# A decode block with TensorE's program in three blocks: all 32 units in its loop, queries by a loop over heads, the last matmuls in block one

## The chip, the cores and the metric

The kernel runs on one core of a Trainium2 chip. A core has five engines that run their own instruction streams and meet at semaphores: TensorE (PE, matmuls; its weight loads are listed as PEld), VectorE (DVE), ScalarE (ACT), GpSimd (POOL) and SyncE (SP), which here issues nearly all transfers from HBM into SBUF. The metric is the device time of one execution in microseconds (us); less is better.

## The reference

One step of decoding for a batch of two: attention over a cache of 8192 keys in 32 heads, and then a gated feed-forward block. All numbers are float32.

```python
# x (2,1,512); k_cache, v_cache (2,32,8192,128); wq (512,4096); wo (4096,512)
# w_gate, w_up (512,1792); w_down (1792,512)
def attention(x, k_cache, v_cache, wq, wo):
    q = (x @ wq).reshape(B, 1, 32, 128).transpose(0, 2, 1, 3)
    scores = einsum("bhqd,bhkd->bhqk", q, k_cache) * 128 ** -0.5
    o = einsum("bhqk,bhkd->bhqd", softmax(scores), v_cache)
    return o.transpose(0, 2, 1, 3).reshape(B, 1, 4096) @ wo
def ffn(x, w_gate, w_up, w_down):
    return (silu(x @ w_gate) * (x @ w_up)) @ w_down
h = x + attention(layernorm(x), k_cache, v_cache, wq, wo)
out = h + ffn(layernorm(h), w_gate, w_up, w_down)
```

## The kernel before, in words

**Units and slots.** The cache is worked through in U = 32 units; a unit is two heads of one batch row, so 8192 KB of keys and 8192 KB of values, laid out as 128 rows of 64 KB. Three SBUF tiles of that size hold them: `kslot0` and `kslot1` for keys in turn, `vslot` for values. Below, k5 means the keys of unit 5 and v5 its values. VectorE multiplies a unit's keys by the query (L471) and sums them to scores (L475), in halves, and takes the maximum (L478). TensorE and ScalarE make the softmax of it (L409 to L413, L502, L506). TensorE multiplies the values by the probabilities `pz` with 32 matmuls into `opart` (L418), ScalarE copies that out (L519), and four more matmuls and a copy give a column of `oT` (L430, L523).

**Who issues what.** The list `loads` is written in the order in which SP issues: wq, k0 (two halves), k1, v0, k2, v1, ... k31, v30, v31, wo (two parts), w_gate, w_up (two parts), w_down (five parts). Before the first part of an item SP waits for what stands in `after`: the release of the tile that the item is written to. `s_kfree` counts units whose keys VectorE has used, `s_vfree` units whose values TensorE has used (ScalarE adds to it, L518). SP issues in order, so whatever stands behind a waiting item waits too. TensorE starts on values when the whole load has landed.

**The last unit.** v30 goes to `vslot` as all values before it. v31 goes to `kslot0` (`v_last`), which is free once VectorE is through with k30. wo follows into `vslot`, after v30 is used; w_gate and w_up go to `kslot1`, after k31; w_down goes to `kslot0`, after v31. For this TensorE's loop has 31 turns, and unit 31 stands behind it as code of its own.

**Queries.** wq lands in `vslot`. The transposed and normalised x (`hT`, 32 columns) is multiplied with it in 32 matmuls (L362), four at a time in four groups of columns; ScalarE copies the two results out (L374); eight matmuls with the constant `picks` (L384) spread them over the partitions, and ScalarE copies each into `qsb` (L397). VectorE starts on k0 after the first of these copies; SP may issue v0 once L362 is through.

**The end.** TensorE multiplies `oq` by wo (32 matmuls, L578), then comes the residual, the second layernorm, w_gate and w_up (L612), and w_down in 14 chunks: eight into `early` (L690), chunks 8 to 13 with four small matmuls each (L658), and four that add `early` (L675). VectorE and ScalarE copy the result out, SP and ScalarE store it.

**Branches of TensorE.** The functions `tour`, `stops`, `far_stop` and `last` write blocks of code to which TensorE jumps at the start (`tour`: to `stop1`, `stop2`, and back to `toured`) or at its end (`back`); they compute nothing.

Of the kernel before, what the change touches and what calls it, by code (L numbers as in the profile page):

```python
# [11 lines left out]
P = 128  # L12
# [42 lines left out]
def decode_block(nc, x, k_cache, v_cache, wq, wo, w_gate, w_up, w_down, out):  # L55
# [43 lines left out]
    quarter = sbuf("quarter", P, NQ)  # L99
    picks = sbuf("picks", P, 2, B, P)  # L100
    om = picks[:, 0].rearrange("p b (h q) -> p b h q", q=NQ)
    sides = sbuf("sides", P, P // (2 * W), 2 * W)
    pz = sbuf("pz", P, NW, 2 * W)
    oT = sbuf("oT", P, H, B)
    hT = sbuf("hT", P, DC, 32)
    osb = sbuf("osb", P, W * DH)
    qsb = sbuf("qsb", P, B, MQ, DH)
    oq = sbuf("oq", P, H, B)
# [36 lines left out]
    def alone(name):  # L145
        return g.sem(name)
# [10 lines left out]

    v_last = kslot[U % 2]

    def load_kv(kind, i, parts=1):  # L160
        cache, t = (k_cache, kslot[i % 2]) if kind == "k" else (v_cache, vslot if i < U - 1 else v_last)
        n = SLOT // parts
        for c in range(parts):
            own = parts > 1 or (kind, i) == ("v", U - 1)
            sem = alone(f"{kind}{i}_{c}") if own else s_k[i % 2] if kind == "k" else s_v
            loads.append(((kind, i), c, t[:, c * n : (c + 1) * n], k_src(cache, i)[:, c * n : (c + 1) * n], sem))
# [8 lines left out]

    wo_t = vslot
    WO = ((0, 20), (20, 12))
# [11 lines left out]
    for e, (c, n) in enumerate(WF):  # L189
# [6 lines left out]
        ))  # L196
    wd_t = v_last
    WD = ((0, 4), (4, 4), (8, 3), (11, 2), (13, 1))
# [8 lines left out]
    for item, e, dst, src, sem in loads:  # L207
        count[sem] = count.get(sem, 0) + 16
        landed[item, e] = (sem, count[sem])
    after = {("v", 0): ("wq", 0), ("wo", 0): ("v", U - 2), ("wf", 0): ("k", U - 1), ("wd", 0): ("v", U - 1)}  # L210
    for i in range(1, U):
        after["v", i] = ("v", i - 1) if i < U - 1 else ("k", U - 2)
        if i > 1:
            after["k", i] = ("k", i - 2)
# [4 lines left out]
    def tour(e):  # L219
        e.br("stop1")  # L220
        never["reg"] = e.alloc_register("never")
        nc.switch_bb("toured", parent=None)

    def stops(e):
        e.br("past1")
        with nc.body("stop1", parent=None, valid_engines=[PE]):
            e.reg_mov(never["reg"], 0)
            never["hint"] = e.mark_branch_hint_location()
            e.br("stop2")
        with nc.body("back", parent=None, valid_engines=[PE]):  # L230
            e.nop()
            e.br("end")
        nc.switch_bb("past1")

    def far_stop(e):
        e.br("past2")
        with nc.body("stop2", parent=None, valid_engines=[PE]):
            e.nop()
            e.br_lt(never["reg"], 1, "toured", "past2").branch_hint(never["hint"])
        nc.switch_bb("past2", parent=None)  # L240

    g.steps["tensor"].append(tour)
    def keep(name, engine):
        held = {}

        def mark(e):
            held["reg"] = e.alloc_register(f"{name}_never")
            e.reg_mov(held["reg"], 0)
            held["at"] = e.mark_branch_hint_location()

# [32 lines left out]
    do("vector", lambda e: e.tensor_reduce(quarter, ident.rearrange("p (q r) -> p q r", q=NQ), axis=AX.X, op=OP.add))  # L283
    for b in range(B):
        do(
            "vector",
            lambda e, b=b: e.tensor_copy(
                picks[:, :, b, :].rearrange("p o (k j) -> p o k j", k=2),
                ident.rearrange("p (o k l) -> p o k l", o=2, k=2)[:, :, :, b : b + 1].to_broadcast([P, 2, 2, HP]),
            ),  # L290
        )
    do("vector", lambda e: e.memset(opart, 0.0))
# [55 lines left out]

    wait("vector", p, consts_done)
    hT_done = do("vector", lambda e: e.tensor_copy(hT[:, :, :B], yt), s_dve)  # L350
    wait("tensor", hT_done, landed[("wq", 0), 0])
    wqv = vslot.rearrange("p (c m k d) -> p c k m d", c=DC, k=2, d=DH)
    raws = (osb, qsb[:, B - 1, MQ - 4 :, :].rearrange("p m d -> p (m d)"))
    q_done = []
    told = []
    for pair, raw in enumerate(raws):
        ps = wide[pair]
        for c in range(DC):
            for t in range(4):
                p = do(  # L360
                    "tensor",
                    lambda e, c=c, t=t, ps=ps, pair=pair: e.matmul(  # L362
                        ps[32 * t : 32 * t + 32, :],
                        hT[:, c, :],
                        wqv[:, c, t % 2, 8 * pair + 4 * (t // 2) : 8 * pair + 4 * (t // 2) + 4, :],
                        start=(c == 0),
                        stop=(c == DC - 1),
                    ),
                    s_pe if c == DC - 1 and t == 3 else None,
                )  # L370
        if pair:
            wqv_read = p
        wait("scalar", p)
        told.append(do("scalar", lambda e, ps=ps, raw=raw: e.activation(raw, ps, AF.Copy), s_act))  # L374
    for n in range(8):
        o, b = divmod(n % 4, B)
        pair, m = n // 4, 4 * (n // B)
        ps = bank[2 * (n % 2)]
        wait("tensor", told[pair])
        if n > 1:  # L380
            wait("tensor", q_done[n - 2])
        p = do(
            "tensor",
            lambda e, o=o, b=b, pair=pair, ps=ps: e.matmul(  # L384
                ps,
                picks[:, o, b, :],
                raws[pair],
                start=True,
                stop=True,
            ),  # L390
            s_pe,
        )
        wait("scalar", p)
        q_done.append(
            do(
                "scalar",
                lambda e, ps=ps, m=m, b=b: e.activation(  # L397
                    qsb[:, b, m : m + 4, :], ps.rearrange("p (j d) -> p j d", d=DH), AF.Copy
                ),
                s_act,  # L400
            )
        )
    freed["wq", 0] = wqv_read
    wait("tensor", q_done[-1])

# [8 lines left out]

    def pe_values(e, t_v):
        for w in range(NW):
            t = w % 4
            inst = e.matmul(  # L418
                opart[32 * t : 32 * t + 2 * W, :],
                pz[:, w, :],  # L420
                t_v[:, w * W * DH : (w + 1) * W * DH],
                start=(w < 4),
                stop=(w >= NW - 4),
            )
        inst.then_inc(s_pe_act, 1)
# [9 lines left out]
    def pe_rounds(e):  # L435
        e.sem_inc(s_v, -16)
        with nc.Fori(0, U - 1, engines=[PE], head_slot={PE: 0}):
            pe_scores(e)
            e.wait_ge(s_v, 16)
            pe_values(e, vslot)  # L440
            pe_outputs(e)
            e.sem_inc(s_dve_pe, -2)
            e.sem_inc(s_act_pe, -2)
            e.sem_inc(s_v, -16)
        stops(e)
        pe_scores(e)
        e.wait_ge(landed[("v", U - 1), 0][0], 16)
        pe_values(e, v_last)
        pe_outputs(e)

    g.steps["tensor"].append(pe_rounds)

# [27 lines left out]
    def dve_rounds(e):  # L480
        dve_unit(e, 0, qsb[:, 0, 0:1, :], True, 0, 0)
        e.wait_ge(*q_done[-1])
        e.sem_inc(s_own_dve, -4)
# [10 lines left out]

    wait("vector", q_done[0])
    g.steps["vector"].append(dve_rounds)
# [101 lines left out]
    h1_done = do("scalar", lambda e: e.activation(h1, attn, AF.Copy), s_act)  # L598
    wait("vector", yt_done)
    hT_done = do("vector", lambda e: e.tensor_copy(hT[:, :, :B], yt), s_dve)  # L600
    wait("tensor", hT_done)

    def project_f(first, ps):
        for c in range(DC):
            for e_, (c0, n) in enumerate(WF):
                if c0 == first + c:
                    wait("tensor", landed[("wf", 0), e_])
            w = wf_t[:, (first + c) * F : (first + c + 1) * F]
# [41 lines left out]
    do("tensor", lambda e: e.matmul(early[:32, :], place, h1, start=True, stop=False))  # L650
    do("tensor", lambda e: e.matmul(opart[:32], hT[:, 0, :], osb, start=True, stop=True))
    wait("tensor", p)
    EARLY = WD[2][0]

    def down(c, t, first):
# [10 lines left out]
        )  # L666

    for c in range(FB):
        if c == WD[3][0]:
            g.steps["tensor"].append(far_stop)  # L670
            wait("tensor", early_done)
# [33 lines left out]

    def last(e):
        e.br_lt(never["reg"], 1, "back", "end").branch_hint(never["back"])
        nc.switch_bb("end", parent=None)

    g.steps["tensor"].append(last)  # L710
    res = rest[:HP, : 2 * P]
# [70 lines left out]
```

## Time and profile before

| what | before |
|---|---|
| time of the runs | 1308.96 us median of 3 (1308.66 to 1309.71) |
| the profiled execution | 1309.24 us, of which the span is 1307.8 us |
| mean granted clock of TensorE | 0.633 of full speed |
| HBM read | 564.66 MB, 432 GB/s over the span |
| busy share | VectorE 87%, TensorE 32%, ScalarE 7%, GpSimd 0% |

A row of the timeline gives start and duration in us, engine, line, operation, the tile written and the tiles read with their shapes (partitions x elements), how many instructions were merged into the row, and in brackets how long the engine had been idle before it and who ended that wait. "SPq" is SP's sequencer, on which a row is the issue of a transfer. In a row on a group of transfers the last number is the median time from issue to landing. In a row on a group of instructions the bar parts the busy time (us) and the mean of one (ns) from the idle time before. A matmul of float32 shows as two passes, so 32 matmuls are x64. L-numbers are those of the code above.

### The profile page before, as it was taken

Reading aid. Unit: us, or ns where it says so; the run is one execution under the profiler, and the core shown is the slowest. Engines: PE = TensorE matmul, PEld = TensorE weight load, DVE = VectorE, ACT = ScalarE, POOL = GpSimd, SP = SyncE. Lnnn points to the kernel's source line nnn. Section 1 sums busy time; section 2 is a strip of 40 time slices with the busy share of each in tenths; the row PEclk is TensorE's granted clock in tenths of the full one; section 3 lists DMA queues with packets and bytes.
Section 4 is the critical chain, followed back from the end, with each engine's and each line's share of the span. In section 5 each row is a group of like instructions: output and inputs, shape, how many; then the busy total and the mean of one; then the engine's idle time right before and its main releaser. Section 6 shows DMA issues by size and latency. Waiting matters only on the chain.

```text
span 1307.8 us, 6699 instructions
## 1 busy us (share of the span) xinstructions
PE 420.2 (32%) x2764; PEld 136.2 (10%) x2764; DVE 1131.2 (87%) x247; ACT 88.0 (7%) x307; POOL 3.1 (0%) x15
## 2 busy tenths in 40 slices
PE   2233223333213333312333321333332233332177
PEld 0010001011001011000101100101100010110022
DVE  0999998899888889888889988888988888998841
ACT  0100000000000000000000000000000000000010
POOL 0000000000000000000000000000000000000000
PEclk9665566666556666556666656666655666665578
DMA  9999999999999999999999999999999999999998
GB/s 403 442 437 435 431 445 421 447 419 447 421 445 421 445 427 441 435 431 445 421 447 419 447 421 445 421 447 427 439 435 431 445 421 447 421 445 421 445 420 370
DMA packets 10959, 564.72 MB, mean 432 GB/s; under 512 B 1222, under 2 KB 1226, under 8 KB 1612
## 3 DMA queue, kind: packets, MB, share of 16 engines
q1 hardware_dynamic: 10948, 564.67, 99.7%
q8 instruction: 3, 0.05, 0.0%
q10 hardware_dynamic: 8, 0.01, 0.0%
HBM read 564.66 MB, written 0.00 MB: 432 GB/s over the span
## 4 chain that ended last, share of the span: by engine, by line
DMA 50%; DVE 48%; PE 2%; issue 0%; ACT 0%; DVEq 0%; SPq 0%; ACTq 0%
DMA kslot<-in_A_k_cache_dram 45%; DVE kslot L471 24%; DVE s L475 24%; DMA kslot<-in_B_w_down_dram 3%; DMA vslot<-in_A_wq_dram 2%; PE opart L418 1%; PE wide L362 1%; DVE gm L456 0%; DVE r L460 0%; SPq L723 0%; PE bank L658 0%; PE bank L384 0%; DVEq L471 0%; ACT pz L506 0%; ACT qsb L397 0%
## 5 line engine op out<-in xcount | busy, mean ns | idle before, releaser
L471 DVE TENSOR_TENSOR kslot<-kslot,qsb 128x8192 f32<-128x8192 f32 x64 | 555.6, 8681 | 118.8 <-DMA kslot<-in_A_k_cache_dram 94.7
L475 DVE TENSOR_REDUCE s<-kslot 128x64 f32<-128x8192 f32 x64 | 555.2, 8675 | 0.1
L418 PE MATMUL opart<-vslot,pz 128*8 128x512 f32 x1984 | 282.8, 734 | 226.5 <-DMA vslot<-in_A_v_cache_dram 226.5
L411 PE MATMUL bank<-gm,nscale 1*128 1x2 f32 x64 | 18.7, 358 | 359.7 <-DVE gm L456 359.7
L418 PEld LDWEIGHTS opart<-vslot,pz 128*8 128x8 f32 x1984 | 55.1, 103 | 428.1 <-DMA vslot<-in_A_v_cache_dram 229.1
L409 PE MATMUL bank<-ident,m 128*1 128x128 f32 x32 | 11.9, 373 | 182.4 <-DVE m L478 182.4
L519 ACT ACTIVATE osb<-opart 128x512 f32<-128x512 f32 x32 | 19.1, 598 | 543.1 <-PE opart L418 543.1
L411 PEld LDWEIGHTS bank<-gm,nscale 1*128 1x128 f32 x64 | 15.9, 307 | 369.1 <-DVE gm L456 369.1
L502 ACT ACTIVATE nb<-bank 64x1 f32<-64x1 f32 x64 | 10.7, 167 | 564.1 <-PE bank L411 563.7
L430 PE MATMUL bank<-rdiag,osb 128*128 128x2 f32 x256 | 34.5, 257 | 40.5 <-ACT rdiag L521 40.5
L430 PEld LDWEIGHTS bank<-rdiag,osb 128*128 128x128 f32 x256 | 31.8, 195 | 70.2 <-ACT rdiag L521 70.2
L413 PE MATMUL bank<-rs,sides 128*128 128x1 f32 x64 | 18.7, 362 | 46.9 <-ACT pz L506 46.9
L506 ACT ACTIVATE pz<-s,nb 64x128 f32<-64x128 f32 x64 | 25.7, 401 | 1.4
L409 PEld LDWEIGHTS bank<-ident,m 128*1 128x1 f32 x32 | 2.5, 79 | 185.8 <-DVE m L478 185.8
L413 PEld LDWEIGHTS bank<-rs,sides 128*128 128x128 f32 x64 | 16.0, 310 | 49.7 <-ACT pz L506 49.7
L478 DVE TENSOR_REDUCE m<-s 128x1 f32<-128x128 f32 x32 | 9.2, 286 | 4.7
L362 PE MATMUL wide<-vslot,hT 128*32 128x512 f32 x64 | 8.4, 685 | 13.2 <-DMA vslot<-in_A_wq_dram 13.2
L298 DVE BATCH_NORM_STATS2 ln_stats<-attn 2x6 f32<-2x512 f32 x1 | 0.7, 687 | 13.0 <-PE attn L591 13.0
L506 ACT ACTIVATION_READ_ACCUMULATOR pz<-s,nb 64x1 f32 x64 | 11.9, 187 | 0.0
L550 DVE TENSOR_TENSOR picks<-oT,quarter 128x256 f32<-128x256 f32 x1 | 0.4, 426 | 11.3 <-ACT oT L523 11.3
L521 ACT ACTIVATE rdiag<-fold,r 128x8 f32<-128x8 f32 x32 | 9.7, 302 | 4.9 <-DVE r L460 4.5
L418 PE MATMUL opart<-kslot,pz 128*8 128x512 f32 x64 | 9.8, 780 | 0.0
(74 smaller groups left out, 92.9 us busy)
## 6 DMA issues: line engine op xcount, KB each, us to landing
kslot<-in_A_k_cache_dram SPq DMA_DIRECT2D x2, 4096.0 KB, 37.2
vslot<-in_A_wo_dram SPq DMA_DIRECT2D x1, 5120.0 KB, 22.1
kslot<-in_B_w_gate_dram SPq DMA_DIRECT2D x1, 3584.0 KB, 31.5
kslot<-in_B_w_up_dram SPq DMA_DIRECT2D x2, 1792.0 KB, 37.3
vslot<-in_A_wo_dram SPq DMA_DIRECT2D x1, 3072.0 KB, 29.0
kslot<-in_B_w_down_dram SPq DMA_DIRECT2D x2, 1024.0 KB, 29.9
kslot<-in_B_w_down_dram SPq DMA_DIRECT2D x1, 768.0 KB, 32.3
kslot<-in_B_w_down_dram SPq DMA_DIRECT2D x1, 512.0 KB, 33.1
```

Of the source, the lines that this page charges most:

```text
L362: lambda e, c=c, t=t, ps=ps, pair=pair: e.matmul(ps[32 * t : 32 * t + 32, :], hT[:, c, :], wqv[:, c, t % 2, 8 * pair + 4 * (t // 2) : 8 * ...
L409: e.transpose(mrow, m1, ident).then_inc(s_pe_dve, 1)
L411: e.matmul(nb_ps, nscale, gm, start=True, stop=True).then_inc(s_pe_act, 1)
L413: e.matmul(den, sides.rearrange("p w a -> p (w a)"), rs, start=True, stop=True).then_inc(s_pe_dve, 1)
L418: inst = e.matmul(opart[32 * t : 32 * t + 2 * W, :], pz[:, w, :], t_v[:, w * W * DH : (w + 1) * W * DH], start=(w < 4), stop=(w >= NW - 4),)
L430: inst = e.matmul(ot_ps, osb[:, a * DH : (a + 1) * DH], rdiag[:, a::W], start=(a == 0), stop=(a == W - 1))
L471: e.tensor_tensor(kt, kt, q.to_broadcast([P, n, DH]), op=OP.mult).then_inc(s_own_dve, 1)
L475: e.tensor_reduce(s[:, c * n : (c + 1) * n], kt, axis=AX.X, op=OP.add).then_inc(s_own_dve, 1)
L502: inst = e.activation(nb[h], nb_ps[h, k : k + 1], AF.Copy)
L506: inst = e.activation(pz[h, :, k * W : (k + 1) * W], s[h].rearrange("p (w a) -> p w a", a=W), AF.Exp, bias=nb[h], scale=SCALE, accum_out=r ...
L519: e.activation(osb, opart, AF.Copy)
L521: e.activation(rdiag, diag, AF.Copy, scale=r).then_inc(s_act_pe, 1)
```

## The change

Three edits that belong together. **The loop.** TensorE's loop takes all 32 units. So v31 goes to `vslot` like the values before it, after v30 is used, wo goes to the key slot `kslot0`, after k30, and w_down to `vslot`, after v31. **Queries.** The transposed x is copied 64 times over into `hrep` (the place of `osb`), so that a matmul with 128 columns gives a query on all the partitions that need it. A loop of four turns does two groups of four matmuls each, into `wide[0]` and `wide[1]`, and ScalarE, in a loop of its own, copies each group with four instructions of 64 x 256 into `qsb`. `picks` and its two VectorE copies go. VectorE starts on k0 when `s_q` is 2 (the first group is copied and TensorE is in its second turn); SP may issue v0 when `s_q` is 5 (all queries are copied). **The end.** Chunks 9 to 13 of w_down and the four matmuls that add `early` are written into a block `late`, which stands in TensorE's program ahead of the loop over units; after chunk 8 TensorE jumps to it by a conditional branch whose hint is given ahead of wo. A single far block `stop` is left for `tour`. The filler matmul into `opart` moves from ahead of w_down to ahead of the second wait for w_up.

```diff
-    v_last = kslot[U % 2]
-
     def load_kv(kind, i, parts=1):
-        cache, t = (k_cache, kslot[i % 2]) if kind == "k" else (v_cache, vslot if i < U - 1 else v_last)
+        cache, t = (k_cache, kslot[i % 2]) if kind == "k" else (v_cache, vslot)
...
-    wo_t = vslot
+    wo_t = kslot[U % 2]
...
-    wd_t = v_last
+    wd_t = vslot
...
-    after = {("v", 0): ("wq", 0), ("wo", 0): ("v", U - 2), ("wf", 0): ("k", U - 1), ("wd", 0): ("v", U - 1)}
+    after = {("v", 0): ("wq", 0), ("wo", 0): ("k", U - 2), ("wf", 0): ("k", U - 1), ("wd", 0): ("v", U - 1)}
     for i in range(1, U):
-        after["v", i] = ("v", i - 1) if i < U - 1 else ("k", U - 2)
+        after["v", i] = ("v", i - 1)
...
     def tour(e):
-        e.br("stop1")
         never["reg"] = e.alloc_register("never")
+        e.reg_mov(never["reg"], 0)
+        never["hint"] = e.mark_branch_hint_location()
+        e.br("stop")
         nc.switch_bb("toured", parent=None)
...
+    def stop(e):
+        e.br("past")
+        with nc.body("stop", parent=None, valid_engines=[PE]):
             e.nop()
-            e.br_lt(never["reg"], 1, "toured", "past2").branch_hint(never["hint"])
-        nc.switch_bb("past2", parent=None)
+            e.br_lt(never["reg"], 1, "toured", "past").branch_hint(never["hint"])
+        nc.switch_bb("past", parent=None)
...
+    h_done = do(
+        "vector", lambda e: e.tensor_copy(hrep, yt[:, :, :, None].to_broadcast([P, DC, B, HP])), s_dve
+    )
+    wait("tensor", h_done, landed[("wq", 0), 0])
+    wqv = vslot.rearrange("p (c m) -> p c m", c=DC)
+    s_q = g.sem("q")
+    Q_FIRST, Q_ALL = (s_q, 2), (s_q, H // 8 + 1)
+
+    def pe_queries(e):
+        e.sem_inc(s_act_pe, 2)
+        with nc.Fori(0, H // 8, engines=[PE]) as i:
+            for k in range(2):
+                e.wait_ge(s_act_pe, k + 1)
+                if k == 0:
+                    e.sem_inc(s_q, 1)
+                for c in range(DC):
+                    inst = e.matmul(
+                        wide[k],
+                        hrep[:, c].rearrange("p b r -> p (b r)"),
+                        wqv[:, c, bass.ds(i * (2 * D) + k * D, D)],
...
+                inst.then_inc(s_pe_act, 1)
+            e.sem_inc(s_act_pe, -2)
+        e.wait_ge(s_act_pe, 2)
+        e.sem_inc(s_act_pe, -2)
+        e.sem_inc(s_q, 1)
+
+    def act_queries(e):
+        with nc.Fori(0, H // 8, engines=[ACT]) as i:
+            for k in range(2):
+                ps = wide[k].rearrange("p (m o d) -> p m o d", o=2, d=DH)
+                e.wait_ge(s_pe_act, k + 1)
+                for b in range(B):
+                    for o in range(2):
+                        inst = e.activation(
+                            qsb[HALF[o], b, bass.ds(i * 4 + 2 * k, 2), :], ps[HALF[b], :, o, :], AF.Copy
+                        )
+                inst.then_inc(s_act_pe, 1)
+            e.sem_inc(s_pe_act, -2)
...
+    freed["wq", 0] = Q_ALL
...
     def pe_rounds(e):
         e.sem_inc(s_v, -16)
-        with nc.Fori(0, U - 1, engines=[PE], head_slot={PE: 0}):
+        e.br("units")
+        with nc.body("late", parent=None, valid_engines=[PE]):
+            for step in late:
+                step(e)
+            e.br("end")
+        nc.switch_bb("units", parent=None)
+        with nc.Fori(0, U, engines=[PE], head_slot={PE: 0}):
             pe_scores(e)
             e.wait_ge(s_v, 16)
-            pe_values(e, vslot)
+            pe_values(e)
             pe_outputs(e)
...
+    def last(e):
+        e.br_lt(never["reg"], 1, "late", "end").branch_hint(never["back"])
+        nc.switch_bb("end", parent=None)
+
     for c in range(FB):
+        if c == EARLY + 1:
+            g.steps["tensor"].append(stop)
+            g.steps["tensor"].append(last)
+            body, g.steps["tensor"] = g.steps["tensor"], late
```

Where instructions stand now shows best in the programs as built. First SP's list at its end, before: the last two loads of values and the weights. `vfree` and `kfree` are `s_vfree` and `s_kfree`.

```order
L723 DMA vslot<-in_A_v_cache_dram 128x16384 [waits vfree]
L723 DMA kslot<-in_A_v_cache_dram 128x16384 [waits kfree]
L723 DMA vslot<-in_A_wo_dram 128x10240 [waits vfree]
L723 DMA vslot<-in_A_wo_dram 128x6144
L723 DMA kslot<-in_B_w_gate_dram 128x7168 [waits kfree]
L723 DMA kslot<-in_B_w_up_dram 128x3584 x2
```

The same place now; the first row stands for both v30 and v31 (x2).

```order
L700 DMA vslot<-in_A_v_cache_dram 128x16384 [waits vfree] x2
L700 DMA kslot<-in_A_wo_dram 128x10240 [waits kfree]
L700 DMA kslot<-in_A_wo_dram 128x6144
L700 DMA kslot<-in_B_w_gate_dram 128x7168 [waits kfree]
L700 DMA kslot<-in_B_w_up_dram 128x3584 x2
```

The order of the items is the same; the wait of v31 is now on `vfree`, and that of wo on `kfree`.

TensorE at the end of its program, before, from the filler matmul (to `opart`) on:

```order
L651 MATMUL opart<-osb,hT 32x512
L690 MATMUL bank<-kslot 32x512 x8
L658 MATMUL bank<-kslot 32x128 x12
L236 UNCONDITIONAL_BRANCH
L239 COMPARE_AND_BRANCH
L675 MATMUL bank<-osb,fold 32x128 x4
L658 MATMUL bank<-kslot 32x128 x12
L707 COMPARE_AND_BRANCH
```

TensorE now, in the middle of its program (ahead of the loop over units, whose first matmul is the last row):

```order
L408 UNCONDITIONAL_BRANCH
L632 MATMUL bank<-vslot,kslot 32x128 x8
L656 MATMUL bank<-osb,fold 32x128 x4
L632 MATMUL bank<-vslot,kslot 32x128 x12
L412 UNCONDITIONAL_BRANCH
L414 ISA
L414 UNCONDITIONAL_BRANCH
L380 MATMUL bank<-ident,m 1x128
```

And at its end:

```order
L625 MATMUL bank<-kslot,place 32x512
L671 MATMUL bank<-vslot,kslot 32x512 x8
L632 MATMUL bank<-vslot,kslot 32x128 x4
L224 UNCONDITIONAL_BRANCH
L227 COMPARE_AND_BRANCH
L643 COMPARE_AND_BRANCH
```

Twenty of the 24 matmuls of chunks 8 to 13, and the four that add `early`, have moved ahead of the loop; TensorE gets to them from the last row.

More of the change, by code (lines that the diff above doesn't have):

```diff
@@ L99, in decode_block @@
     quarter = sbuf("quarter", P, NQ)
-    picks = sbuf("picks", P, 2, B, P)
-    om = picks[:, 0].rearrange("p b (h q) -> p b h q", q=NQ)
+    om = sbuf("om", P, B, H, NQ)
     sides = sbuf("sides", P, P // (2 * W), 2 * W)
@@ L106, in decode_block @@
     osb = sbuf("osb", P, W * DH)
+    hrep = osb.rearrange("p (c b r) -> p c b r", c=DC, b=B)
     qsb = sbuf("qsb", P, B, MQ, DH)
@@ L156, in k_src @@
         return cache[b, 2 * m : 2 * m + 2].rearrange("h (p j) d -> (h p) (j d)", p=HP)
-    v_last = kslot[U % 2]
     def load_kv(kind, i, parts=1):
-        cache, t = (k_cache, kslot[i % 2]) if kind == "k" else (v_cache, vslot if i < U - 1 else v_last)
+        cache, t = (k_cache, kslot[i % 2]) if kind == "k" else (v_cache, vslot)
         n = SLOT // parts
         for c in range(parts):
-            own = parts > 1 or (kind, i) == ("v", U - 1)
-            sem = alone(f"{kind}{i}_{c}") if own else s_k[i % 2] if kind == "k" else s_v
+            sem = alone(f"{kind}{i}_{c}") if parts > 1 else s_k[i % 2] if kind == "k" else s_v
             loads.append(((kind, i), c, t[:, c * n : (c + 1) * n], k_src(cache, i)[:, c * n : (c + 1) * n], sem))
@@ L219, in tour @@
     def tour(e):
-        e.br("stop1")
         never["reg"] = e.alloc_register("never")
+        e.reg_mov(never["reg"], 0)
+        never["hint"] = e.mark_branch_hint_location()
+        e.br("stop")
         nc.switch_bb("toured", parent=None)
[L224 to L230, printed above, removed]
-            e.nop()
[L232 to L238, printed above, removed]
-            e.br_lt(never["reg"], 1, "toured", "past2").branch_hint(never["hint"])
-        nc.switch_bb("past2", parent=None)
+    def stop(e):
+        e.br("past")
+        with nc.body("stop", parent=None, valid_engines=[PE]):
+            e.nop()
+            e.br_lt(never["reg"], 1, "toured", "past").branch_hint(never["hint"])
+        nc.switch_bb("past", parent=None)
     g.steps["tensor"].append(tour)
@@ L283, in decode_block @@
     do("vector", lambda e: e.tensor_reduce(quarter, ident.rearrange("p (q r) -> p q r", q=NQ), axis=AX.X, op=OP.add))
[L284 to L291, printed above, removed]
     do("vector", lambda e: e.memset(opart, 0.0))
@@ L346, in decode_block @@
     consts_done = p0
[L349 to L365, printed above, removed]
+    wait("vector", p)
@@ L366, in decode_block @@
                         start=(c == 0),
                         stop=(c == DC - 1),
[L368 to L402, printed above, removed]
@@ L403, in decode_block @@
-    freed["wq", 0] = wqv_read
-    wait("tensor", q_done[-1])
+                    )
[13 more added lines that the diff above has]
+                            qsb[HALF[o], b, bass.ds(i * 4 + 2 * k, 2), :], ps[HALF[b], :, o, :], AF.Copy
+                        )
+                inst.then_inc(s_act_pe, 1)
+            e.sem_inc(s_pe_act, -2)
@@ L407, in pe_scores @@
+    g.steps["tensor"].append(pe_queries)
+    g.steps["scalar"].append(act_queries)
+    freed["wq", 0] = Q_ALL
     def pe_scores(e):
@@ L413, in pe_scores, with pe_values @@
         e.matmul(den, sides.rearrange("p w a -> p (w a)"), rs, start=True, stop=True).then_inc(s_pe_dve, 1)
-    def pe_values(e, t_v):
+    def pe_values(e):
         for w in range(NW):
@@ L420, in pe_values @@
                 pz[:, w, :],
-                t_v[:, w * W * DH : (w + 1) * W * DH],
+                vslot[:, w * W * DH : (w + 1) * W * DH],
                 start=(w < 4),
@@ L444, in pe_rounds @@
             e.sem_inc(s_v, -16)
[L445 to L449, printed above, removed]
+    late = []
     g.steps["tensor"].append(pe_rounds)
@@ L481, in dve_rounds @@
         dve_unit(e, 0, qsb[:, 0, 0:1, :], True, 0, 0)
-        e.wait_ge(*q_done[-1])
+        e.wait_ge(*Q_ALL)
         e.sem_inc(s_own_dve, -4)
@@ L493, in dve_rounds @@
         recip(e, 4)
-    wait("vector", q_done[0])
+    wait("vector", Q_FIRST)
     g.steps["vector"].append(dve_rounds)
@@ L598, in decode_block @@
     h1_done = do("scalar", lambda e: e.activation(h1, attn, AF.Copy), s_act)
-    wait("vector", yt_done)
+    wait("vector", yt_done, consts_done)
     hT_done = do("vector", lambda e: e.tensor_copy(hT[:, :, :B], yt), s_dve)
@@ L606, in project_f @@
                 if c0 == first + c:
+                    if c:
+                        do("tensor", lambda e: e.matmul(opart[:32], hT[:, 0, :], osb, start=True, stop=True))
                     wait("tensor", landed[("wf", 0), e_])
@@ L650, in decode_block @@
     do("tensor", lambda e: e.matmul(early[:32, :], place, h1, start=True, stop=False))
-    do("tensor", lambda e: e.matmul(opart[:32], hT[:, 0, :], osb, start=True, stop=True))
     wait("tensor", p)
@@ L666, in down @@
         )
+    def last(e):
+        e.br_lt(never["reg"], 1, "late", "end").branch_hint(never["back"])
+        nc.switch_bb("end", parent=None)
     for c in range(FB):
+        if c == EARLY + 1:
+            g.steps["tensor"].append(stop)
+            g.steps["tensor"].append(last)
+            body, g.steps["tensor"] = g.steps["tensor"], late
         if c == WD[3][0]:
-            g.steps["tensor"].append(far_stop)
             wait("tensor", early_done)
@@ L704, in decode_block @@
             p = down(c, t, c == EARLY)
[L706 to L710, printed above, removed]
+    g.steps["tensor"] = body
     res = rest[:HP, : 2 * P]
```

## The prediction

> **What bounds the kernel now.** I read the page first: busy shares, DMA queues, then the chain of waits.
>
> ```profile
> span 1307.8 us, 6699 instructions
> PE 420.2 (32%) x2764; PEld 136.2 (10%) x2764; DVE 1131.2 (87%) x247; ACT 88.0 (7%) x307; POOL 3.1 (0%) x15
> q1 hardware_dynamic: 10948, 564.67, 99.7%
> q8 instruction: 3, 0.05, 0.0%
> DMA 50%; DVE 48%; PE 2%; issue 0%; ACT 0%; DVEq 0%; SPq 0%; ACTq 0%
> ```
>
> SP's queue moves 564.67 MB and is at work 99.7% of the span. The chain names VectorE almost as often as DMA, but the chain in order of time shows which one gives the pace:
>
> ```profile
> 1067.49 8.69 DVE kslot L471
> 1144.77 8.69 DVE kslot L471
> 1179.65 42.24 DMA kslot<-in_A_k_cache_dram
> 1221.92 8.69 DVE kslot L471
> 1271.75 33.15 DMA kslot<-in_B_w_down_dram
> 1304.95 1.11 PE bank L658 x24
> L475 DVE TENSOR_REDUCE s<-kslot 128x64 f32<-128x8192 f32 x64 | 555.2, 8675 | 0.1
> ```
>
> The rows at 1067.49 and 1144.77 are the same instruction two units apart: 77.28 us for four loads, so 19.32 us a load, though VectorE has only two multiplies (L471) and two sums (L475), 4 x 8.7 = 34.8 us, in the 38.64 us of a unit. From 1179.65 on the end is transfers: keys, then the last piece of w_down, then 1.1 us of TensorE. So the question for each edit is whether SP's queue ever runs dry.
>
> The timeline of the last two units shows how the queue is kept full:
>
> ```profile
> 1212.47 0.33 SPq L723 DMA_DIRECT2D vslot<-in_A_v_cache_dram  x1
> 1218.24 0.33 SPq L723 DMA_DIRECT2D kslot<-in_A_v_cache_dram  x1
> 1241.22 9.21 PE L418 MATMUL opart<-vslot,pz 128*8 128x512 f32 x64 [7.73 <-DMA vslot<-in_A_v_cache_dram]
> 1250.54 0.80 SPq L723 DMA_DIRECT2D vslot<-in_A_wo_dram  x2
> 1250.59 0.60 ACT L519 ACTIVATE osb<-opart 128x512 f32<-128x512 f32 x1 [17.75 <-PE opart L418]
> 1260.53 9.79 PE L418 MATMUL opart<-kslot,pz 128*8 128x512 f32 x64
> 1270.43 2.92 SPq L723 DMA_DIRECT2D kslot<-in_B_w_down_dram  x5
> 1274.56 9.60 PE L578 MATMUL wide<-vslot,oq 128*2 128x512 f32 x64 [0.40 <-ACT oq L568]
> kslot<-in_A_v_cache_dram SPq DMA_DIRECT2D x1, 42.2
> vslot<-in_A_wq_dram SPq DMA_DIRECT2D x1, 23.4
> ```
>
> Values of unit 30 (v30) are issued at 1212.47 and land at 1241.2, when L418 starts on them. The last values, v31, were issued at 1218.24, into a key slot, and waited behind v30: the queue goes from one into the other, and v31 lands at 1218.24 + 42.2 = 1260.44. When v30 is used up (1250.5) ScalarE frees the slot and SP issues wo, still 10 us ahead of v31's landing.
>
> **The change part by part.** *wo takes the key slot, v31 the value slot.* SP's list keeps its order (v30, v31, wo), but v31 now waits for v30's slot, and wo, w_gate, w_up and w_down stand behind it on SP. wo's own wait (unit 30's keys, free at 1218.24) is then long met. Between the landing of v30 (1241.2) and its release (1250.54) nothing is left in the queue: VectorE, which frees the key slots, can't help, since SP stands at v31. So the queue runs dry, and v31 starts from an idle queue at 1250.54.
>
> How long it then takes is shown once, at the start, by wq, also 8 MB in 128 rows, with other loads behind it:
>
> ```profile
> 0.74 0.41 SPq L723 DMA_DIRECT2D vslot<-in_A_wq_dram  x1
> 24.31 8.41 PE L362 MATMUL wide<-vslot,hT 128*32 128x512 f32 x64 [13.15 <-DMA vslot<-in_A_wq_dram]
> 0.73 0.55 ACTq L262 DMA_DIRECT2D xs<-in_A_x_dram  x1
> 2.96 0.62 DVE L298 BATCH_NORM_STATS2 ln_stats<-xs 2x6 f32<-2x512 f32 x1
> ```
>
> 23.4 us from issue to landing, 4.1 more than the 19.32 of a load in the stream. So v31 lands at 1250.54 + 23.4 = 1273.9 in place of 1260.4: 13.5 us late. The lower bound is the small load of x: issued at 0.73, used at 2.96, thus at most 2.2 us besides its bytes. With it v31 lands at 1250.54 + 2.2 + 19.32 = 1272.1, 11.6 us late. Nothing can be below 1250.54 + 19.32, 9.4 us late. I take 13.5, from wq, the same load from the same state. [...]
>
> All that comes after moves with v31. The queue behind it is the same bytes in the same order: w_down's last piece landed at 1304.9, 44.5 us after v31. TensorE's chain does too: values at 1260.53, wo at 1274.56, 14.0 us later, waiting for nothing but v31. w_down's issue moves with the end of v31's values; it still has the bytes of wo, w_gate and w_up ahead of it. So the 13.5 us reach the end whole.
>
> *Unit 31 inside the loop.* One more turn of TensorE's loop stands while TensorE waits for v31 anyway, at no cost; that cover is now larger.
>
> *Queries by a loop.* 32 matmuls of 128 columns replace 32 of 32 columns that ran four at a time, and 8 picking matmuls. The nearest rows:
>
> ```profile
> L384 PE MATMUL bank<-osb,picks 128*128 128x512 f32 x8 | 3.8, 618 | 0.0
> 32.77 0.33 SPq L723 DMA_DIRECT2D vslot<-in_A_v_cache_dram  x1
> 34.44 8.69 DVE L471 TENSOR_TENSOR kslot<-kslot,qsb 128x8192 f32<-128x8192 f32 x1 [23.08 <-ACT qsb L397]
> 69.26 0.33 SPq L723 DMA_DIRECT2D kslot<-in_A_k_cache_dram  x1
> 82.13 8.49 PE L418 MATMUL opart<-vslot,pz 128*8 128x512 f32 x64 [0.82 <-DMA vslot<-in_A_v_cache_dram]
> ```
>
> L384: four matmuls of this size in 3.8 us, waits on ScalarE included, so 0.95 each at most; 32 of them 30.4 us at most, and queries end by 24.3 + 30.4 = 54.7, plus a last copy. v0, which waits for them, has until the queue's backlog is gone: it lands at 82.1, so k1 lands about 62.8, and 4.1 us of start before that is 58.7. Covered. VectorE may start after the first group of four matmuls and its four copies, about 30, before the first half of k0 lands (24.2 + 9.7 = 33.8), where 34.44 was bound by the query: 0.6 us earlier, which gains nothing, since VectorE waits for keys later. Late, it would be harmless up to 8.6 us: k2, issued at 69.26, must be in the queue 4.1 us before v0's landing. Cost zero; the cover is the backlog of keys.
>
> *Constants.* Two VectorE copies fewer, a wider copy of the transposed rows, all before wq lands at 24.2: zero. Fewer program blocks: the profile shows three instruction fetches, 0.05 MB, in q8; even all of them are 0.1 us of the queue. Zero. The filler matmul moves into a wait of TensorE: zero.
>
> *End of w_down in block one.* After the four matmuls of chunk 8 TensorE jumps backward.
>
> ```profile
> 1303.66 0.86 PE L658 MATMUL bank<-kslot 128*32 128x128 f32 x24 [0.80 <-DMA kslot<-in_B_w_down_dram]
> 1304.34 0.40 PE L675 MATMUL bank<-osb,fold 128*32 128x128 f32 x8
> 1304.95 1.06 PE L658 MATMUL bank<-kslot 128*32 128x128 f32 x24 [0.21 <-DMA kslot<-in_B_w_down_dram]
> 140.21 0.06 DVEq L484
> 140.30 0.17 DVEq L484
> 140.47 0.28 issue
> 140.84 0.07 DVEq L471
> ```
>
> The only cover there is the 0.21 us wait for the last pieces. A branch taken back is seen on VectorE's loop: 140.30 to 140.75, about 0.5 us. Bounds 0 (the sequencer runs ahead of the matmuls) and 0.5; I take 0.3.
>
> **Sum.** 13.5 + 0.3 = 13.8 us. The profiled execution took 1309.24 us (1.4 more than its span); 1309.24 + 13.8 = 1323.0. The median of the runs lies 0.28 lower, so 1322.8.
>
> **Rivals.**
> - *Short restart.* The 4.1 us of wq belong to the start of a program, not to an idle queue. For it: x's 2.2 us. Against it: wq is the only large load seen from idle. 11.6 + 0.3 = 11.9, so 1320.9 for the median. [...]
> - *The jump misses.* The late block isn't at hand, and TensorE waits for its code while the output hangs on it.
>
> ```profile
> 4.63 0.55 DVE L308 TENSOR_SCALAR ln_y<-xs,ln_mv,ln_rstd 2x512 f32<-2x512 f32 x1 [0.67 <-POOL ln_rstd L304]
> 10.55 0.61 PE L316 MATMUL bank<-ident,ln_y 2*128 2x2 f32 x4 [10.55 <-issue]
> ```
>
>   L316 could have started at 5.2; TensorE, touring through two far blocks, came at 10.55. Three jumps in 9.8 us are 3.3 each, up to 4.9 if two were fetches. [...] 13.5 + (3.3 to 4.9) - 0.2: 1325.6 to 1327.2. [...]
> - *The other side: not slower.* The reload of the queue must cost nothing: v30's slot would have to be free before v30's last bytes land, or the tail after v31 would have to hold 13.5 us that isn't transfer. It decides at 1241.2: if TensorE used up v30 as it arrived, the wait would be met and the time would be 1309. Against it: L418 starts on v30 only when the whole load has landed, and needs 9.2 us. That the change doesn't do what it says (fewer blocks) would leave the 13.5 us as they are.
>
> **How the numbers follow.** Forecast 0.62, short restart 0.23, missed jump 0.11, not slower 0.02, anything else 0.02. Forecast and short restart alone span 1320 to 1323.5; to hold 8 in 10 with the unknown of the jump I go from 1319.3 (restart below x's bound) to 1326.0. A measurement tells about 0.2% (2.6 us) from no change; all cases but the last are slower by more: slower 0.97, same 0.02, faster 0.01.
>
> **What would show it.** After the change: SP's issue of the last values near 1250.5, not 1218.2, and wo right behind; a hole in the DMA rate from 1241 to about 1253; L418's last group (now on vslot) starting near 1274; the last piece of w_down landing near 1318.4; VectorE's first multiply near 33.9. Wrong I'd be if the list of loads were issued in another order, if the rate after the hole were above 19.3 us a load, or if TensorE showed a gap of microseconds after chunk 8.

## The result and the profile after

The changed kernel takes 1320.88 us (median of 6 runs, 1320.01 to 1321.54), the kernel before in the same rounds 1309.24: a ratio of 1.0088, with a 95% interval of 1.0075 to 1.0101. It is 11.6 us slower; 13.8 us more and 1322.8 us were forecast. The profiled execution took 1321.31 us, 12.07 more than that of before, and its span is 12.2 longer.

The page of the profile after, span and queues:

```profile
span 1320.0 us, 6797 instructions
q1 hardware_dynamic: 10948, 564.67, 98.9%
q8 instruction: 2, 0.03, 0.0%
q14 instruction: 1, 0.01, 0.0%
```

The bytes are the same, and the queue's share falls from 99.7% to 98.9%: by these shares some 3.9 us without work became 14.5. The fetches of program code are still three (q8 and q14). The chain in order of time shows where the time lies (start, duration, what):

```profile
1212.36 28.70 DMA vslot<-in_A_v_cache_dram
1241.10 9.27 PE opart L389 x64
1250.43 22.03 DMA vslot<-in_A_v_cache_dram
1272.50 8.93 PE opart L389 x64
1281.88 31.90 DMA vslot<-in_B_w_down_dram
1313.83 1.93 PE bank L671 x8
1315.76 1.53 PE bank L632 x24
1317.29 0.23 PE bank L656 x8
1317.52 0.71 PE bank L632 x24
1318.25 0.28 DVE kslot L692
```

v30 lands at 1241.1, TensorE uses it, and only then v31 starts; it lands at 1272.46, where it landed at 1260.44 before: 12.0 us late. SP stands at v31 for 38 us (the first row below has v30's issue and v31's), and wo goes out right behind it. The timeline of SP and TensorE:

```profile
1212.36 38.40 SPq L700 DMA_DIRECT2D vslot<-in_A_v_cache_dram  x2
1250.80 0.91 SPq L700 DMA_DIRECT2D kslot<-in_A_wo_dram  x2
1272.50 8.88 PE L389 MATMUL opart<-vslot,pz 128*8 128x512 f32 x64 [12.05 <-DMA vslot<-in_A_v_cache_dram]
```

The same by stages of 10 us; the last three columns are TensorE's granted clock, the DMA share and GB/s:

```profile
1230.00:1240.00 10.00, 1.17 (x4) 0.99 (x4) 10.00 (x4) 1.31 (x6) 0.00 (x0) 0.50 0.74 321
1240.00:1250.00 10.00, 8.90 (x64) 1.79 (x64) 10.00 (x3) 0.00 (x0) 0.00 (x0) 0.72 0.00 0
1250.00:1260.00 10.00, 2.46 (x16) 1.68 (x12) 7.15 (x3) 2.56 (x10) 0.00 (x0) 0.79 1.02 413
```

A whole stage has a DMA share of 0.00. In windows of 0.2 us the records of the queue's packets stop at 1239.6, 1.5 us before TensorE starts on v30, and begin again at 1251.2, 0.8 us after v31's issue: a hole of 11.6 us. The groups and rows of the new query stage:

```profile
L347 PE MATMUL wide<-vslot,osb 128*128 x64 | 30.8, 646 | 16.0 <-PEq L340 16.0
31.29 1.28 ACT L367 ACT_TABLE_LOAD   x1 [31.29 <-PE wide L347]
34.25 8.69 DVE L444 TENSOR_TENSOR kslot<-kslot,qsb 128x8192 f32<-128x8192 f32 x1 [24.87 <-PEq L345]
57.41 0.33 SPq L700 DMA_DIRECT2D vslot<-in_A_v_cache_dram  x1
```

Queries take 30.8 us of TensorE. v0 is issued at 57.41, 1.3 us before the forecast's limit of 58.7. TensorE starts on v0 at 82.04; it was 82.13 before.

### The profile page after: what moved, and what is told of

It reads as the page before. It is cut to its first block, busy times and chain, and to the rows that moved or that the text cites. A ratio compares the mean times of both kernels' runs of the same rounds, so it can differ in the third digit from the quotient of the medians.

```text
span 1320.0 us, 6797 instructions
## 1 busy us (share of the span) xinstructions
PE 434.2 (33%) x2748; PEld 144.2 (11%) x2748; DVE 1131.4 (86%) x245; ACT 97.6 (7%) x332; POOL 3.1 (0%) x15
## 3 DMA queue, kind: packets, MB, share of 16 engines
q1 hardware_dynamic: 10948, 564.67, 98.9%
## 4 chain that ended last, share of the span: by engine, by line
DMA 73%; PE 23%; issue 0%; ACTq 0%; SPq 0%; DVE 0%; PEldq 0%
DMA vslot<-in_A_v_cache_dram 70%; PE opart L389 22%; DMA vslot<-in_B_w_down_dram 2%; PE bank L632 0%; PE bank L671 0%; ACTq L491 0%; SPq L700 0%; DVE kslot L692 0%; PE bank L656 0%; PEldq L358 0%
## 5 line engine op out<-in xcount | busy, mean ns | idle before, releaser
L389 PE MATMUL opart<-vslot,pz 128*8 128x512 f32 x2048 | 293.5, 738 | 239.0 <-DMA vslot<-in_A_v_cache_dram 239.0
L347 PE MATMUL wide<-vslot,osb 128*128 x64 | 30.8, 646 | 16.0 <-PEq L340 16.0
L347 PEld LDWEIGHTS wide<-vslot,osb 128*128 128x128 f32 x64 | 12.9, 207 | 33.2 <-issue 33.2
L367 ACT ACTIVATE qsb<-wide 64x256 f32 x32 | 12.1, 378 | 2.8 <-PE wide L347 2.4
```

What stands on the lines that cost most here:

```text
L347: inst = e.matmul(wide[k], hrep[:, c].rearrange("p b r -> p (b r)"), wqv[:, c, bass.ds(i * (2 * D) + k * D, D)], start=(c == 0), stop=(c = ...
L367: inst = e.activation(qsb[HALF[o], b, bass.ds(i * 4 + 2 * k, 2), :], ps[HALF[b], :, o, :], AF.Copy)
L389: inst = e.matmul(opart[32 * t : 32 * t + 2 * W, :], pz[:, w, :], vslot[:, w * W * DH : (w + 1) * W * DH], start=(w < 4), stop=(w >= NW - 4),)
```

## The experiments

The theory: the whole loss is SP's queue standing empty, 9.3 us until v30 is used up and then a restart. The first rivals: the query loop or the jump carry a part, or the tail behind v31 is not rigid.

**The loop and the tiles alone.** The kernel before, with its loop and tiles changed as in the changed kernel and nothing else (in excerpts, as all diffs below):

```diff
-        with nc.Fori(0, U - 1, engines=[PE], head_slot={PE: 0}):
+        with nc.Fori(0, U, engines=[PE], head_slot={PE: 0}):
...
         stops(e)
-        pe_scores(e)
-        e.wait_ge(landed[("v", U - 1), 0][0], 16)
-        pe_values(e, v_last)
-        pe_outputs(e)
...
-    wo_t = vslot
+    wo_t = kslot[U % 2]
...
-    wd_t = v_last
+    wd_t = vslot
...
-        after["v", i] = ("v", i - 1) if i < U - 1 else ("k", U - 2)
+        after["v", i] = ("v", i - 1)
```

> The kernel before with the loop and the tiles alone changed: 32 units in TensorE's loop, v31 to the value slot, wo to the key slot, w_down to the value slot; queries and the end of w_down as before. Gap theory (the whole loss is the dry queue: 9.3 us from the landing of v30 to its release, plus 2.7 us of restart): 1309.2 + 12.0 = 1321.2 us, v31 issued near 1250.5 and landing 22.0 us later. Rival (the new query loop or the jump to the late block carry part of it): less by their part, below 1319 if they carry 2 us.

Measured: 1321.45 us against 1309.16, ratio 1.0095 (1.0079 to 1.0110). Its chain:

```profile
1240.98 9.94 PE opart L415 x64
1250.98 21.77 DMA vslot<-in_A_v_cache_dram
```

The whole loss is there with the queries and the end of before.

**The other two edits alone.** The changed kernel with v31 back in the key slot:

```diff
-    wo_t = kslot[U % 2]
+    wo_t = vslot
...
-        after["v", i] = ("v", i - 1)
+        after["v", i] = ("v", i - 1) if i < U - 1 else ("k", U - 2)
...
-        with nc.Fori(0, U, engines=[PE], head_slot={PE: 0}):
+        with nc.Fori(0, U - 1, engines=[PE], head_slot={PE: 0}):
...
+        pe_scores(e)
+        e.wait_ge(landed[("v", U - 1), 0][0], 16)
+        pe_values(e, v_last)
+        pe_outputs(e)
```

> The changed kernel with the tiles and the loop of 31 put back (v31 to the key slot after k30, wo to the value slot, unit 31 as code of its own), the query loop and the late block kept. Gap theory: 1309.2 us, within 0.5 of before, v31 issued near 1218 and landing near 1260.4. Rival (query loop or late block cost time): 1310.5 to 1313, with a gap at the jump after chunk 8, or a hole in the DMA rate near 58 to 82 us because v0 is issued too late.

Measured: 1309.42 us against 1309.16 (11 and 15 runs), ratio 1.0000 (0.9991 to 1.0009). From its timeline:

```profile
1218.48 0.33 SPq L707 DMA_DIRECT2D kslot<-in_A_v_cache_dram  x1
1260.77 9.06 PE L392 MATMUL opart<-kslot,pz 128*8 128x512 f32 x64
1304.03 1.65 PE L639 MATMUL bank<-kslot 128*32 128x128 f32 x24
1305.46 0.58 PE L663 MATMUL bank<-osb,fold 128*32 128x128 f32 x8
```

Query loop and late block change nothing that these runs can tell: at most 0.1%, or 1.2 us. The jump lies behind the first eight of the 24 passes at 1304.03, and the row has no room for a gap of microseconds: it is as long as in the changed kernel (1.65 us at 1315.64, at a mean granted clock of 0.54 from 1315.7 to 1317.3), and in the kernel before 24 passes with no jump among them took 0.86 us at 1.0 (1303.66), twice which is 1.72. The two kernels together account for the change.

**Half of wo ahead of v31.**

```diff
-    load_kv("v", U - 1)
...
-    WO = ((0, 20), (20, 12))
+    WO = ((0, 16), (16, 16))
...
+        if e == 0:
+            load_kv("v", U - 1)
```

> The changed kernel with the first half of wo (4 MB, 9.6 us of transfer, to the key slot that is free by then) issued ahead of v31, so that the queue has work while v30 is used up. If the loss is lost transfer time only: 1309.5 us. My theory has two paths, the bytes and the chain of TensorE behind v31: v31 lands 9.7 us late, near 1270.1, the queue itself ends near 1305, but the chain behind v31 had only about 2 us of slack before, so 1309.2 + 9.7 - 2 = 1316.9 us, with TensorE no longer waiting for w_down.

Measured: 1315.42 us against 1309.16, ratio 1.0049 (1.0033 to 1.0064). So giving the queue most of its work back doesn't give the time back: half the loss stays. From its timeline:

```profile
1250.77 0.33 SPq L701 DMA_DIRECT2D vslot<-in_A_v_cache_dram  x1
1272.52 9.19 PE L390 MATMUL opart<-vslot,pz 128*8 128x512 f32 x64 [12.07 <-DMA vslot<-in_A_v_cache_dram]
1308.22 1.92 PE L672 MATMUL bank<-vslot,kslot 128*32 128x512 f32 x16 [0.84 <-DVE kslot L624]
1311.10 0.84 PE L633 MATMUL bank<-vslot,kslot 128*32 128x128 f32 x24
```

No matmul of w_down waits for a transfer any more; the chain of TensorE behind v31 sets the end. The mechanism was right and two sizes were off. First, v31 came at 1272.5 and not at 1270.1, 21.7 us after its issue, a whole restart. Half of wo takes 9.7 us in the stream and would land at 1250.8, just when v31 is issued, but that is too late to bridge: the packet records stop at 1249.4 and begin again at 1251.6 (windows of 0.2 us). The 10 us from 1240, below, move only 370 GB/s. Second, TensorE's chain without waits for transfers is 39.4 us (1272.5 to 1311.9) where 45.6 stood before, a slack of 6 us and not 2. Of this the waits for transfers are 2.3 us (0.96, 0.29, 0.80 and 0.21 in the kernel before); another 2.6 us is wo's matmuls, which took 7.05 us; before they took 9.60, at a granted clock of 0.52 over the first 5.4 us and 1.0 after that.

```profile
1240.00:1250.00 10.00, 8.88 (x60) 1.80 (x64) 10.00 (x3) 0.00 (x0) 0.00 (x0) 0.69 0.86 370
```

**v31 in halves.** A semaphore tells SP when TensorE has used the first half of v30.

```diff
+            if w == NW // 2 - 1:
+                inst.then_inc(s_half, 1)
...
+        if (item, e_) == (("v", U - 1), 0):
+            wait("sync", (s_half, U - 1))
```

> The changed kernel with v31 loaded in two halves, the first as soon as TensorE has used the first half of v30. Gap theory: the dry time falls from 9.3 to about 4.8 us (TensorE's first 16 matmuls are at the lower clock), the restart of 2.7 stays: 7.5 us over before, 1316.7 us, 4.3 less than the changed kernel. If the loss were a fixed price of issuing v31 behind v30: 1320.9 as now.

Measured: 1317.51 us against 1308.94, ratio 1.0064 (1.0047 to 1.0081): 8.6 over before, where 7.5 were expected and 12 stood. From its timeline:

```profile
1247.02 0.33 SPq L710 DMA_DIRECT2D vslot<-in_A_v_cache_dram  x1
1268.97 9.02 PE L393 MATMUL opart<-vslot,pz 128*8 128x512 f32 x64 [7.74 <-DMA vslot<-in_A_v_cache_dram]
```

The first half went out at 1247.02, 6.0 us after v30's landing (1241.06) and not 4.8; with a restart of 2.7 that makes 8.7. The loss follows the dry time.

**Two loads swapped in mid-stream.** The kernel before, with v15 ahead of k16:

```diff
-        load_kv("k", i)
-        load_kv("v", i - 1)
+        for kind, n in (("v", i - 1), ("k", i)) if i == U // 2 else (("k", i), ("v", i - 1)):
+            load_kv(kind, n)
```

> The kernel before with one pair of loads swapped in the middle of the stream: v15 stands ahead of k16 in SP's list, so SP waits for the release of v14 with nothing behind it in the queue. Gap theory (a dry queue costs the dry time plus a restart wherever it is, since the queue gives the pace of the whole stream): about 9.3 + 2.7 = 12 us more, 1321 us, v15 landing 22 us after its issue. Rival (VectorE's reserve of 3.9 us a unit, or the 15 units behind, take it up): 1309 to 1312.

Measured: 1325.07 us against 1308.94, ratio 1.0122 (1.0105 to 1.0139): 16.1 us, neither of the two. VectorE's reserve doesn't take it up, and 4 us came on top. The timeline and a window of it:

```profile
632.91 0.33 SPq L723 DMA_DIRECT2D vslot<-in_A_v_cache_dram  x1
674.18 8.69 DVE L471 TENSOR_TENSOR kslot<-kslot,qsb 128x8192 f32<-128x8192 f32 x1 [35.15 <-DMA kslot<-in_A_k_cache_dram]
685.67 9.19 PE L418 MATMUL opart<-vslot,pz 128*8 128x512 f32 x64
694.98 0.33 SPq L723 DMA_DIRECT2D vslot<-in_A_v_cache_dram  x1
692.00:694.00 2.00, 2.00 (x24) 0.50 (x20) 2.00 (x1) 0.00 (x0) 0.00 (x0) 1.00 0.00 0
```

The maximum that unit 15's softmax needs stands on VectorE behind the first multiply of unit 16, which waited 35 us for k16. So TensorE used v15 late, v16 was issued at 694.98, and the queue stood empty a second time. That this second hole is the 4 us is the next run's question.

**One hole and no swap.** To test that, k16 alone is held until v14 is used; the order stays.

```diff
+        if item == ("k", U // 2):
+            wait("sync", freed["v", U // 2 - 2])
```

> The kernel before with k16 also held until v14 is used, the order of the loads unchanged: the queue runs dry once in mid-stream, as in the swapped pair, but VectorE gets k16 first. Theory: the swap cost 16 us, 12 for the dry queue and 4 for a second dry stretch, since softmax of unit 15 stood behind k16 on VectorE and v16 was issued 1 us after the queue had emptied. Here only the first is left: 1309.0 + 12.0 = 1321.0 us, one hole in the DMA rate. Rival (a hole in mid-stream costs 16 us by itself): 1325.

Measured: 1321.74 us against 1309.14, ratio 1.0094 (1.0078 to 1.0109): 12.6 us. Its chain has the same restart, on keys, in the middle of the stream, and the second hole is gone:

```profile
632.25 21.85 DMA kslot<-in_A_k_cache_dram
692.00:694.00 2.00, 0.00 (x0) 0.00 (x0) 1.07 (x1) 0.00 (x0) 0.00 (x0) 0.50 1.00 426
```

A dry queue costs about the same 690 us from the end as 70 us from it: 12.6 us here, 12.3 with the loop and the tiles alone.

**The first loads held back.** The kernel before with one wait ahead of SP's list:

```diff
+    wait("sync", hT_done)
     wait("tensor", hT_done, landed[("wq", 0), 0])
```

> The kernel before with all of SP's loads held back until VectorE has copied the transposed x (about 11.4 us). It tells what made wq take 23.4 us from issue to landing where v31 took 22.0. If it is the traffic and set-up of the program's first microseconds: wq lands 22.0 us after its issue, and the time is 1309.2 + 10.7 - 1.4 = 1318.5 us. If it belongs to wq (its tensor, or the loads behind it): 23.4 us again, and 1319.9 us.

Measured: 1314.98 us against 1308.94, ratio 1.0044 (1.0028 to 1.0060). Neither expected time came, since the loads went out at 7.17 and not at 11.4. The chain of this run:

```profile
7.17 21.73 DMA vslot<-in_A_wq_dram
29.03 8.87 PE wide L363 x64
```

wq now takes 21.7 us, near v31's 22.0, and not 23.4 (23.06 to 23.44 in four profiles in which it is issued at 0.74). So the extra belongs to the first microseconds of the program and not to a restart; which of the things that run there makes it (x, program code, tables) these runs don't tell apart. The issue came at 7.17, not at 11.4, since TensorE reached its transposes at 6.33 in place of 10.55. The sum with these numbers is 6.43 - 1.71 = 4.7; the profiled execution took 4.8 more than that of before (1314.01 and 1309.24), the median of three runs 6.0 more (1314.98); the 1.3 us between these are not explained.

**The filler matmul put back.**

```diff
-                    if c:
-                        do("tensor", lambda e: e.matmul(opart[:32], hT[:, 0, :], osb, start=True, stop=True))
...
+    do("tensor", lambda e: e.matmul(opart[:32], hT[:, 0, :], osb, start=True, stop=True))
```

> The changed kernel with the filler matmul put back ahead of w_down. In the profile after, TensorE's granted clock is 0.5 from 1314 to 1317 (1.0 in the kernel before), and TensorE works without a wait from 1313.8 to the end. If the moved filler is the reason and costs the end: the clock stays at 1.0 there, the last four matmuls wait for the last piece, and the time is 0.3 to 1.0 us less than the changed kernel's 1320.9, about 1320.2. Rival (the transfers set that end anyway, the clock is only a mark): 1320.9, within 0.2.

Measured: 1321.42 us (1320.18 to 1322.43), ratio 1.0096 (1.0080 to 1.0111). The second group of w_down is quick again:

```profile
1312.88 1.06 PE L670 MATMUL bank<-vslot,kslot 128*32 128x512 f32 x8 [0.37 <-DMA vslot<-in_B_w_down_dram]
```

It took 1.93 us in the changed kernel, at a granted clock of 0.50. In the kernel before, where the filler stands at this place too, it took 1.06 at 1.00 (1301.80). From the start of this group to the copy of the result it is 4.2 us here and 4.4 in the changed kernel, so the moved filler costs some 0.2 us in the profiles. The times can't show that, nor the 0.3 us that were the least expected: four runs spread over 2.2 us. So the rival is likely by the two profiles, not shown by the times.

**TensorE kept busy ahead of the values.** If the dry time is TensorE's on v30, a higher clock should shorten it: in the changed kernel the granted clock is 0.5 until 1245.5, 4.4 us after TensorE starts on v30, and 1.0 after that.

```diff
+            for n in range(14):
+                e.matmul(wide[1], sides.rearrange("p w a -> p (w a)"), qsb[:, 0, 0:4, :], start=True, stop=True)
             e.wait_ge(s_v, 16)
```

> The changed kernel with 14 filler matmuls (128 x 512, constant operands, a bank that is free) in each turn of TensorE's loop, ahead of the wait for the values. So TensorE works when the values land, and should have the full clock for all of them. Theory: the dry time is TensorE's time on v30; it was 9.2 us in the profile after (8.4 to 9.9 in the profiles of four kernels), with the first part at a granted clock of 0.5. At full clock the 16 sets of matmuls take 0.43 us each, 6.9 us; the dry time falls by 2.3 us and the time to 1318.6 us, with runs closer together. Rival (the dry time is not TensorE's, or the restart grows as it shrinks): 1320.9. If the fillers overrun the landing, a little more than 1318.6.

Measured: 1330.49 us against 1309.14, ratio 1.0162 (1.0149 to 1.0176). I had sized the fillers wrongly: they took 14.5 us a turn (465.2 us in 32 turns) in a wait of 7.7, so the values began some 7 us late in every turn, and the run doesn't test the theory. With six:

> The same with 6 fillers in place of 14, since 14 took 14.3 us (0.43 us a pass at full clock, two passes each, 2.3 us more for the part at half clock) where TensorE waits only 7.7 us for the values; 6 take about 7.4. In the run with 14 the matmuls on the values took 7.05 us, but began late. Theory: L389 on v30 begins at the landing and takes 7.1 us in place of 9.2, the dry time falls to 7.3 us, and the time to 1318.8 us. Rival (the dry time isn't TensorE's time on v30): 1320.9.

Measured: 1320.34 us against 1308.81, ratio 1.0087 (1.0073 to 1.0101). Its timeline:

```profile
1233.55 8.43 PE L417 MATMUL wide<-qsb,sides 128*128 128x512 f32 x12
1241.90 7.05 PE L389 MATMUL opart<-vslot,pz 128*8 128x512 f32 x64
```

The values take 7.05 us and not 9.2, but the fillers still overran by 0.5 (v30 landed 31.4 us after its issue at 1209.99, thus at 1241.4). v31 went out 1.4 us earlier than in the changed kernel and landed 1.7 us earlier, but the span is only 0.8 us shorter. The ratio can't be told from 1.0088, so the gain of 2 us is not shown in the time; where the rest of v31's lead went stays open.

## Why the prediction was right, and where its size was off

- *The place and the sign.* Right: v31 issued at 1250.4 (1250.5 forecast), wo right behind, no byte moved from 1240 to 1250, and the loss comes with this edit alone and goes with it alone.
- *The dry time.* 9.3 us forecast and measured (1241.1 to 1250.4). The hole in the DMA rate lies elsewhere than I wrote, 1239.6 to 1251.2 and not 1241 to 1253.
- *The restart.* This term was mis-sized. I took wq's 23.4 us, 4.1 over a load in the stream; it is 22.03 us here, 21.8 with the tiles alone and 21.9 in mid-stream, thus 2.4 to 2.7 over 19.32. The rival of the short restart, with x's 2.2 us, was nearer: 1320.9 against 1320.88 measured. That it fits to 0.02 us is luck: v31 came 12.0 us late and not 11.6, and the median lies 0.4 us below the profiled execution and not 0.28. wq was the same load from the same empty queue, but in another state of the program; the run with the first loads held back shows that 1.7 us of it was that state.
- *All of it reaches the end.* Right in sum: v31 was 12.0 us late and the span 12.2 longer. The run with half of wo ahead shows that this holds by two paths, the bytes and TensorE's chain, of which the second has 6 us of slack. One row I read wrongly: before, TensorE began on v31 at 1260.53 not for v31, which had landed 0.1 us earlier, but behind the softmax of unit 31, and the chain of waits from 1221.92 to there is VectorE's and the softmax's, not transfers. The two paths were level, so the sum doesn't change.
- *The jump.* 0.3 us forecast; the kernel with queries and late block alone is within 0.1% of before, which can't tell 0.3 us from nothing. The missed jump didn't come: chunk 8 to the end is one unbroken chain of TensorE above. The bound of 0 has a forward branch of the kernel before for it: L236 stands between the passes at 1303.66, whose row ends at 1304.52, and L675, which starts at 1304.34. The missed jump's price of 3.3 to 4.9 us was not that of the jumps alone: I took it from L316 at 10.55, and with the first loads held back L316 came at 6.33 behind the same two far blocks. No run shows what TensorE waited for there, or what the hint ahead of wo does.
- *Queries at no cost.* Right, though the bound was none: TensorE took 30.8 us, 0.96 us a matmul, against "30.4 at most", which I had from a row of eight passes in 3.8 us. The cover held with 1.3 us to spare, and more with the shorter restart. VectorE started at 34.25, not at 33.9: the first four matmuls took 6.7 us and not 3.8, and ScalarE's table load of 1.28 us, which now stands in its loop, I hadn't counted. Either alone would have been over before the keys landed. (k2's reserve is 8.7 us by the numbers given, not 8.6.)

## What to carry to other kernels

Before moving a load to another tile, look at what its new wait leaves in the issuing queue: an in-order queue that waits for the use of the load just landed has nothing to move, and where transfers set the pace it costs the time of use plus a restart, in the two places tried. To price a restart, don't take the first transfer of a program. And before filling such a hole with other work, follow the chain behind the load that is put off, and let the filling reach past the issue of that load: here half the loss stayed.

## What the runs showed that I had not expected

- Most of a restart is time at the two ends of the hole. Of the 2.7 us, 1.5 lie between the last packet record (1239.6) and TensorE's start on v30 (1241.1), and 0.8 between v31's issue (1250.4) and the first packet record (1251.2). In the kernel before the packets of the next load go on through this time: the queue's share is 100% from 1205 to 1260.
- TensorE's time on the same 32 matmuls of v30 was 8.4, 9.2, 9.3, 9.5 and 9.9 us in the profiles of five kernels, by how much of it ran at the granted clock of 0.5 (until 1243.7 in the fastest, with 8.4, by the spacing of its weight loads; until 1245.5 in the changed kernel, with 9.2). While the queue stayed full this was hidden; here it is in the dry time. Whether it also makes the runs spread is not shown: with six fillers (7.05 us) five runs lie within 0.5 us, where six of the changed kernel spread over 1.5 and four with the filler put back over 2.2, but with 14 fillers, 7.05 us too, five spread over 1.3.
- A float32 pass with 128 columns and 512 elements, two to a matmul, took 0.43 us at a granted clock of 1.0 (queries of the changed kernel, from 30.6 on), and twice that, 0.86, the six fillers' first passes. Four passes on the values, of 8 columns each, show the same two times: 0.43 us at 1.0, and 0.85 at 0.5 (the changed kernel on v30). The first seven passes of the queries took 0.86 too, though the record of the granted clock says 1.0 there; why is open. With these and the waits between the groups the 32 matmuls came to 30.8 us.
